# Three moves in the last stage of an adaLN block: the range check's passes, one norm among the gelus, and the order of eight transposes

## The chip, the cores and the metric

The kernel runs on one core of one Trainium2 chip. The metric is the device time of one execution in microseconds (us). One execution was also taken by the hardware profiler; its span, from the first to the last instruction, and all durations below come from that one.

Engines are named as in the profile: PE is TensorE's matmul, PEld its weight load, DVE is VectorE, ACT is ScalarE, POOL is GpSimd, SP is SyncE, which here issues most of the DMAs.

## The reference, cut to what matters

One transformer block with adaptive layer norm, for one sequence of 2048 tokens, width 512, 32 heads of 16, and an MLP of width 1376, all in bf16:

```python
sa, ca, ga, sb, cb, gb = (silu(c) @ w_mod).reshape(6, 512)
h = layernorm(x) * (1 + ca) + sa
q, k, v = split_heads(h @ wqkv)                  # 32 heads of 16
p = softmax(q @ k.T * 16 ** -0.5)
x = x + ga * (merge_heads(p @ v) @ wo)
h = layernorm(x) * (1 + cb) + sb
x = x + gb * (gelu(h @ w1 + b1) @ w2 + b2)
```

## The kernel before, in words

Attention fills nearly all of the time. The 2048 queries are taken in four blocks of 512, and in each block the heads in pairs. Scores, exponentials and the product with V are put in an order by a planner that runs while the kernel is written out: it keeps a clock for each of PE, ACT, DVE and POOL and gives the engine that is free first its next piece. It has nothing to say about the part that is changed here: after its loop (lines 1551 to 1590) the last tokens are finished by the function `last_tail` (line 1602), in an order written out by hand. Each engine runs its own instructions in the order in which they are written, so the order of the lines is the order of each engine's queue.

`last_tail` deals with the last block of 512 tokens. Its first 256 tokens ("first half", columns `hA`) have had their attention, residual and norm already; what is left of them is the MLP. Its last 256 tokens ("second half", `hB`, two tiles of 128 tokens) still need everything from the last head pair's softmax division on. The function weaves the two together:

- `fillers` (line 1623) is a generator with the first half's MLP. Eleven times `up_one` (four matmuls of 256 columns and a gelu on ACT), each followed by two steps of the generator; then 22 "downs", single matmuls of 512 columns, eleven for each of the two tiles of tokens, one a step. `gap(n)` advances it by n steps: n steps in the first phase are n/2 ups, in the second phase n downs. The list `GAPS` (line 101) says how many steps go into each of the places, `GAPS[3]` those just ahead of the second half's norm.
- The second half's residual sums lie in two PSUM banks, `pz[0]` and `pz[1]`. Their mean and variance go to DVE (lines 1661 to 1663) and the root to POOL (`ln_root`, lines 291 and 292). Then (1667 to 1672) DVE works out `nb`, ACT normalizes tile 1 (`hns[1]`, an Identity activation) and DVE tile 0 (`hns[0]`).
- Eight PE transposes (1674 to 1677) turn both tiles into banks `kd` and `kr`: chunk j of tile i. Before the change the loop over j is the outer one. ACT copies chunks 0 and 1 to `h2` (1678), DVE chunks 2 and 3 (1679), which are the input of the second half's ups.
- `gap(GAPS[4])`, then DVE copies the residual sums from PSUM to `xr` (1681, 1682).
- The second half's eleven `up_one` (1683 to 1686), in the middle of which `gap(GAPS[6])` puts 13 fillers; `gap(99)` (1687) puts whatever fillers are left.
- `out_add(0)` and `out_add(1)` (1694): DVE adds the residual of the first half, and SP stores the two tiles.
- `range_flag()` (1696, body from 1711): five passes on DVE over `dall`, which holds all the softmax denominators, reduce it to a column `bad`. PE multiplies `bad` by a column of ones (1697), DVE makes a flag of it (1698), and after the tail a general path is run if the flag isn't zero. With these inputs it isn't run.
- The second half's downs: eleven matmuls for tile 2 into `pz[0]` (1699), and for tile 3 two column halves, each one matmul by the identity for the residual and eleven of 256 columns (1703 to 1709). DVE and ACT copy the results, SP and ACT's queue store them.

The five passes of the range check are these (a sixth DVE instruction, line 1721, sets the column of ones):

```python
nc.vector.tensor_scalar(out=ok, in0=dall, scalar1=2.0 ** 30, scalar2=None, op0=ALU.is_le)      # 1713
nc.vector.scalar_tensor_tensor(out=ok, in0=dall, scalar=256.0, in1=ok, op0=ALU.is_ge, op1=ALU.mult)
nc.vector.tensor_reduce(out=okr, in_=ok, axis=mybir.AxisListType.XY, op=ALU.min)               # 1717
nc.vector.tensor_scalar(out=bad, in0=okr, scalar1=-1.0, scalar2=1.0, op0=ALU.mult, op1=ALU.add)
nc.vector.memset(onec, 1.0)                                                                    # 1721
```

The last row of `dall` comes in by the DMA of line 1660, early in the tail.

Of the kernel before, what the change touches and what calls it, by code (L numbers as in the profile page):

```python
# [26 lines left out]
NC = 4  # L27
# [70 lines left out]
TIE = True  # L98
SEARCH = None
NARROW = False  # L100
GAPS = (4, 2, 2, 17, 2, 3, 13)
NHQ = 4
N2_ENG = DV
NHC = NC - NHQ // 2
# [59 lines left out]
def adaln_block(ctx: ExitStack, tc: tile.TileContext, A_x, A_wqkv, A_wo, B_x, B_w1, B_b1, B_w2, B_b2,  # L164
# [81 lines left out]
    def bank(i):  # L246
        return PS[:, i, :]
# [41 lines left out]
    def ln_root(mv, n):  # L289
        rs = small.tile([P, 4], FP32, name="rs")  # L290
        nc.gpsimd.tensor_scalar(out=rs[:, 0:n], in0=mv[:, 0:n, 1], scalar1=EPS, scalar2=None, op0=ALU.add)  # L291
        nc.gpsimd.tensor_tensor(out=rs[:, 0:n], in0=rs[:, 0:n], in1=mhalf[:, 0:n], op=ALU.pow)
        return rs
# [36 lines left out]
    def copy(eng, dst, src):  # L330
        if eng == AC:
            nc.scalar.copy(out=dst, in_=src)
        else:
            nc.vector.tensor_copy(out=dst, in_=src)
# [1267 lines left out]
    def last_tail():  # L1602
# [13 lines left out]
        def up_one(fc, k, half):  # L1616
            ps = bank(k)[:, 0:256]
            for j in range(NC):
                up_mm(ps, h2 if half else ha, fc, j, hB if half else hA)
            nc.scalar.activation(out=uG[:, fc, hB] if half else ua(fc), in_=ps, func=ACT.Gelu_apprx_tanh, bias=b1c[:, fc:fc + 1],  # L1620
                                 scale=1.0)
# [13 lines left out]
        def gap(n):  # L1635
            for _ in range(n):
                next(gen, None)

        nc.vector.tensor_copy(out=o, in_=bank(kO))
        nc.scalar.activation(out=onec, in_=onec, func=ACT.Gelu_apprx_tanh)  # L1640
        gap(GAPS[0])
        cols = [slice(P * i, P * i + P) for i in range(4)]
# [3 lines left out]
        nc.vector.reciprocal(out=rt.rearrange("p t r -> p (t r)"), in_=bank(kd)[:, 0:16])  # L1646
        gap(GAPS[1])
        for i in (0, 2, 1, 3):
            nc.vector.tensor_copy(out=rx[:, cols[i]].rearrange("p (r e) -> p r e", e=32),
                                  in_=rt[:, i, :].unsqueeze(2).to_broadcast([P, 4, 32]))  # L1650
            nc.tensor.matmul(out=bank(kr)[:, cols[i]], lhsT=rx[:, cols[i]], rhs=ident32, start=True, stop=True)
        gap(GAPS[2])
        for t in range(2):
# [10 lines left out]
        rs = ln_root(mv, 2)  # L1664
        gap(GAPS[3])
        nb = small.tile([P, 2], FP32, name="nb")
# [4 lines left out]
        nc.vector.tensor_scalar(out=hns[0], in0=bank(pz[0]), scalar1=mv[:, 0, 0:1], scalar2=rs[:, 0:1],  # L1671
                                op0=ALU.subtract, op1=ALU.mult)
        both = [PS[:, k, :].bitcast(BF16).rearrange("p (j n) -> p j n", n=256) for k in (kd, kr)]
        for j in range(NC):
            for i in range(2):
                nc.tensor.transpose(out=both[j // 2][:, j, i * P:(i + 1) * P], in_=hns[i][:, j * P:(j + 1) * P],
                                    identity=ident)
        copy(AC, h2[:, 0:2, hB], both[0][:, 0:2, :])
        copy(DV, h2[:, 2:4, hB], both[1][:, 2:4, :])
        gap(GAPS[4])  # L1680
        for t in range(2):
            copy(DV, xr[:, 2 + t, :], bank(pz[t]))
        for fc in range(NFC):
            up_one(fc, (kO, kw, kd, kr)[fc % 4], 1)
            if fc == GAPS[5]:
                gap(GAPS[6])
        gap(99)

        def out_add(tt, k):
            obs[tt] = tl2.tile([P, D], BF16, name="ob")  # L1690
            nc.vector.tensor_tensor(out=obs[tt], in0=bank(k), in1=xr[:, tt, :] if tt > 1 else xa[:, tt, :], op=ALU.add)
            (nc.scalar if tt == 3 else nc.sync).dma_start(out=out_tok[4 * b + tt], in_=obs[tt])

        for tt in range(2):
            out_add(tt, dA[tt])
        bad, onec_, fl = range_flag()
        nc.tensor.matmul(out=bank(kw)[0:1, 0:1], lhsT=bad, rhs=onec_, start=True, stop=True)
        nc.vector.tensor_copy(out=fl, in_=bank(kw)[0:1, 0:1])
        for fc in range(NFC):
# [11 lines left out]
    def range_flag():  # L1711
        ok = odp.tile([P, 512], FP32, name="rb").rearrange("p (q f) -> p q f", f=16)
        nc.vector.tensor_scalar(out=ok, in0=dall, scalar1=2.0 ** 30, scalar2=None, op0=ALU.is_le)
        nc.vector.scalar_tensor_tensor(out=ok, in0=dall, scalar=256.0, in1=ok,
                                       op0=ALU.is_ge, op1=ALU.mult)
        okr = gp.tile([P, 1], FP32, name="okr")
        nc.vector.tensor_reduce(out=okr, in_=ok, axis=mybir.AxisListType.XY, op=ALU.min)
        bad = gp.tile([P, 1], BF16, name="bad")
        nc.vector.tensor_scalar(out=bad, in0=okr, scalar1=-1.0, scalar2=1.0, op0=ALU.mult, op1=ALU.add)
        onec = gp.tile([P, 1], BF16, name="onec")  # L1720
        nc.vector.memset(onec, 1.0)
        fl = gp.tile([1, 1], I32, name="fl")
        late.update(fl=fl)
        return bad, onec, fl
# [104 lines left out]

    scr_d1 = scr.tile([4, 512], FP32, name="d1")  # L1830
    last_tail()
    att.close()
    general_path()
# [35 lines left out]
```

## Time and profile before

| what | us |
|---|---|
| median of 3 runs (lowest to highest) | 757.19 (755.67 to 757.39) |
| the profiled execution's own time | 755.64 |
| its span, first to last instruction | 753.9 |
| PE busy in the span | 734.1 (97%) |
| ACT busy | 721.2 (96%) |
| DVE busy | 676.5 (90%) |
| POOL busy | 415.6 (55%) |
| last exponential of the attention ends | 721.1 |
| `last_tail`'s first instruction starts (DVE, line 1639) | 721.58 |
| last matmul ends | 750.30 |

The profile's rows name an instruction by the line that writes it, its engine, its operation and the tiles it writes and reads (`out<-in`). A line may be that of a helper: all ups and downs of the tail carry line 689, the helper `plain`, and are told apart by their operands: `hT,W` is an up of the first half, `h2T,W` one of the second, `W,hT` a down of the first half, `W,uG` one of the second. Line 1620 is the gelu (`hT` first half, `uG` second), lines 332 and 334 are `copy` on ACT and DVE, line 1691 is `out_add`'s addition, L1676 the transposes. Times are us from the span's start. The duration of a matmul includes the time that its result takes to come out; matmuls that follow each other closely overlap, so that their spacing, start to start, is shorter than their duration.

### The profile page before, as it was taken

Reading aid. Unit: us, or ns where it says so; the run is one execution under the profiler, and the core shown is the slowest. Engines: PE = TensorE matmul, PEld = TensorE weight load, DVE = VectorE, ACT = ScalarE, POOL = GpSimd, SP = SyncE. Lnnn points to the kernel's source line nnn. Section 1 sums busy time; section 2 is a strip of 40 time slices with the busy share of each in tenths; the row PEclk is TensorE's granted clock in tenths of the full one; section 3 lists DMA queues with packets and bytes.
Section 4 is the critical chain, followed back from the end, with each engine's and each line's share of the span. In section 5 each row is a group of like instructions: output and inputs, shape, how many; then the busy total and the mean of one; then the engine's idle time right before and its main releaser. Section 6 shows DMA issues by size and latency. Waiting matters only on the chain.

```text
span 753.9 us, 22023 instructions
## 1 busy us (share of the span) xinstructions
PE 734.1 (97%) x9010; PEld 238.2 (32%) x9010; DVE 676.5 (90%) x1185; ACT 721.2 (96%) x779; POOL 415.6 (55%) x263
## 2 busy tenths in 40 slices
PE   8999999999999999999999999999999999999996
PEld 3322322232333222222222222222222223444454
DVE  6958999999999999899999999999999989898832
ACT  4999999999999999999999999999999999999971
POOL 4103556566675655766556677765756466345700
PEclk9999999999999999999999999999999999999998
DMA  9400000021110110000100200001100200010110
GB/s 318 116 16 2 25 10 17 8 91 38 45 50 10 30 24 18 3 23 23 45 17 18 37 3 17 14 13 30 45 17 9 45 3 17 9 43 19 38 17 31
DMA packets 41964, 25.60 MB, mean 34 GB/s; under 512 B 26705, under 2 KB 37010, under 8 KB 41858
## 3 DMA queue, kind: packets, MB, share of 16 engines
q1 hardware_dynamic: 41042, 23.02, 12.1%
q8 instruction: 72, 1.18, 0.6%
q10 hardware_dynamic: 816, 1.12, 0.4%
q14 instruction: 34, 0.28, 0.1%
HBM read 16.59 MB, written 2.61 MB: 25 GB/s over the span
## 4 chain that ended last, share of the span: by engine, by line
ACT 50%; PE 38%; issue 9%; DVE 1%; POOL 1%; DMA 0%; DVEq 0%; ACTq 0%; POOLq 0%
ACT pB L1300 24%; ACT pA L1300 24%; PE PS L1108 13%; PE PS L944 13%; PE PS L254 8%; PE PS L689 3%; ACT uG L749 1%; POOL t L1348 1%; DMA xb<-in_A_x_dram 0%; PE PS L1125 0%; ACT hT L1620 0%; ACT L1300 0%; DVE st L281 0%; PE PS L311 0%; ACT hT L321 0%
## 5 line engine op out<-in xcount | busy, mean ns | idle before, releaser
L1348 POOL TENSOR_SCALAR t<-t 128x2048 int16<-128x2048 int16 x187 | 353.9, 1901 | 257.5 <-DVE t L1342 149.7
L1300 ACT ACTIVATE pA<-PS 128x1024 bf16<-128x1024 f32 x369 | 395.9, 1073 | 2.6 <-PE PS L944 2.4
L1300 ACT ACTIVATE pB<-PS 128x1024 bf16<-128x1024 f32 x369 | 396.1, 1073 | 0.2
L1371 DVE TENSOR_SCALAR t<-PS 128x512 int16<-128x512 f32 x572 | 369.5, 681 | 25.0 <-PE PS L944 21.1
L944 PE MATMUL PS<-qm,kT 32*128 32x512 bf16 x2048 | 307.5, 383 | 6.7 <-ACT pA L1300 2.7
L1108 PE MATMUL PS<-t,VV 128*32 128x512 f16 (+1 forms) x1944 | 226.9, 359 | 2.5 <-POOL t L1348 1.4
L944 PEld LDWEIGHTS <-kT 32*128 32x128 bf16 x2048 | 85.3, 91 | 289.1 <-issue 285.5
L1342 DVE TENSOR_SCALAR t<-t 128x2048 int16<-128x2048 int16 x242 | 173.0, 742 | 0.5
L1108 PE MATMUL PS<-pA,VE 128*32 128x512 bf16 (+1 forms) x828 | 170.4, 361 | 0.0
L1108 PE MATMUL PS<-pB,VE 128*32 128x512 bf16 (+1 forms) x828 | 166.1, 361 | 0.0
L1108 PE MATMUL PS<-t,VE 128*32 128x512 f16 (+1 forms) x648 | 133.6, 359 | 0.2 <-DVE t L1371 0.2
L1108 PEld LDWEIGHTS <-VE 128*32 128x32 bf16 x2304 | 69.7, 94 | 76.8 <-issue 70.5
L1108 PEld LDWEIGHTS <-VV 128*32 128x32 bf16 x1944 | 64.6, 95 | 55.1 <-issue 50.6
L254 PE MATMUL PS<-h2T,W 128*32 128x512 bf16 x528 | 42.7, 383 | 0.0
L254 PE MATMUL PS<-W,uG 128*32 128x512 bf16 x528 | 41.3, 383 | 0.0
L1125 PE MATMUL PS<-kT,zeros 128*32 128x512 bf16 x288 | 27.8, 383 | 0.0
L341 DVE TENSOR_SCALAR qm<-PS,qmask 128x512 bf16<-128x512 f32 x32 | 22.5, 742 | 3.4 <-PE PS L254 3.4
L740 DVE TENSOR_SCALAR uG<-PS,b1c 128x512 bf16<-128x512 f32 x33 | 24.5, 742 | 1.1 <-PE PS L254 1.1
L1486 POOL TENSOR_TENSOR OT<-o_sb,rb 128x512 bf16<-128x512 f32 (+1 forms) x17 | 20.1, 1179 | 9.4 <-DVE t L1342 7.1
L291 POOL TENSOR_SCALAR rs<-mv 128x4 f32<-128x4 f32 (+1 forms) x10 | 4.3, 432 | 34.8 <-DVE mv L286 34.7
L254 PE MATMUL PS<-hT,W_k 128*32 128x512 bf16 x256 | 20.8, 383 | 1.0 <-DVE hT L324 0.9
L254 PE MATMUL PS<-hT,W_q 128*32 128x512 bf16 x256 | 20.5, 383 | 0.0
(142 smaller groups left out, 376.7 us busy)
## 6 DMA issues: line engine op xcount, KB each, us to landing
rb<-d SPq DMA_DIRECT2D x112, 32.0 KB
W_m<-in_w_mod_dram SPq DMA_DIRECT2D x2, 1024.0 KB
out_dram<-ob SPq DMA_DIRECT2D x15, 128.0 KB
o_sb<-o SPq DMA_DIRECT2D x56, 32.0 KB
xb<-in_A_x_dram SPq DMA_DIRECT2D x3, 512.0 KB
xr<-in_A_x_dram SPq DMA_DIRECT2D x3, 512.0 KB
W<-in_B_w_dram SPq DMA_DIRECT2D x4, 344.0 KB
W<-in_B_w_dram SPq DMA_DIRECT2D x5, 256.0 KB
```

The source lines that it names most:

```text
L254: nc.tensor.matmul(out=ps[32 * g:32 * g + 32, :], lhsT=lhsT[:, 32 * g:32 * g + 32], rhs=rhs, start=start, stop=stop)
L341: nc.vector.tensor_scalar(out=qm[(b, ch)][:, par, :], in0=ps, scalar1=qmask[:, par:par + 1], scalar2=None, op0=ALU.mult)
L689: nc.tensor.matmul(out=ps, lhsT=lhsT, rhs=rhs, start=start, stop=stop)
L740: nc.vector.tensor_scalar(out=X["u"][:, fc, :], in0=bank(ps), scalar1=late["b1c"][:, fc:fc + 1], scalar2=None, op0=ALU.add)
L944: nc.tensor.matmul(out=dst, lhsT=kT[rows, ch, kt * P:(kt + 1) * P], rhs=rhs, start=True, stop=True)
L1108: nc.tensor.matmul(out=bank(O[qi])[32 * r:32 * r + 32, cs], lhsT=w, rhs=rhs[:, cs], start=(n == 1 and not halved(qi)), stop=last and (pr = ...
L1125: nc.tensor.matmul(out=bank(O[qi])[32 * r:32 * r + 32, :], lhsT=zeros[:, 0:32], rhs=kT[:, 0, 0:512], start=False, stop=False)
L1300: nc.scalar.activation(out=t[:, 0:n, :], in_=PS[:, b0:b0 + n, :], func=ACT.Exp, scale=math.log(2.0) / STEP)
L1342: nc.vector.tensor_scalar(out=t16[:, rs, :], in0=d["tile"][:, rs, :], scalar1=float(MJ[j]), scalar2=None, op0=ALU.add)
L1348: nc.gpsimd.tensor_scalar(out=t16[:, rs, :], in0=d["tile"][:, rs, :], scalar1=1.0, scalar2=float(MJ[j]), op0=ALU.mult, op1=ALU.add)
L1371: nc.vector.tensor_scalar(out=d["tile"][:, r:r + n, :], in0=PS[:, i:i + n, :], scalar1=T_BIAS, scalar2=0.0, op0=ALU.add, op1=ALU.max)
L1486: nc.gpsimd.tensor_tensor(out=ot[:, 0:w], in0=o[:, 0:w], in1=rb[:, 0:w], op=ALU.mult)
```

## The change

The fillers ahead of the second half's norm go from 17 steps to 12, and a new gap of 4 steps stands between the norm and the transposes. The loop over the two tiles becomes the outer one in the transposes. `range_flag()` is called after the residual's copies, ahead of the second half's ups, and no longer after `out_add(1)`; the matmul with `bad` stays where it was.

```diff
-GAPS = (4, 2, 2, 17, 2, 3, 13)
+GAPS = (4, 2, 2, 12, 2, 3, 13, 4)
...
         nc.vector.tensor_scalar(out=hns[0], in0=bank(pz[0]), scalar1=mv[:, 0, 0:1], scalar2=rs[:, 0:1],
                                 op0=ALU.subtract, op1=ALU.mult)
         both = [PS[:, k, :].bitcast(BF16).rearrange("p (j n) -> p j n", n=256) for k in (kd, kr)]
-        for j in range(NC):
-            for i in range(2):
+        gap(GAPS[7])
+        for i in range(2):
+            for j in range(NC):
                 nc.tensor.transpose(out=both[j // 2][:, j, i * P:(i + 1) * P], in_=hns[i][:, j * P:(j + 1) * P],
                                     identity=ident)
...
         for t in range(2):
             copy(DV, xr[:, 2 + t, :], bank(pz[t]))
+        bad, onec_, fl = range_flag()
         for fc in range(NFC):
             up_one(fc, (kO, kw, kd, kr)[fc % 4], 1)
...
         for tt in range(2):
             out_add(tt, dA[tt])
-        bad, onec_, fl = range_flag()
         nc.tensor.matmul(out=bank(kw)[0:1, 0:1], lhsT=bad, rhs=onec_, start=True, stop=True)
```

Counted out in steps of the generator: before, 8 steps are taken by the first three gaps (ups 0 to 3), 17 by the gap ahead of the norm (ups 4 to 10 and downs 0 to 2), then 2, 13 and the last 4. After, the gap of 12 takes ups 4 to 9, the new gap of 4 takes up 10 and downs 0 and 1, then come 2, 13 and the last 5. So on ACT the norm of tile 1 stands ahead of the gelu of up 10, where it stood behind it, and one down of 22 moves from ahead of the transposes to the last gap.

## The prediction

> **What bounds the kernel now.** I read the page first, then the chain of work that ended last from 715 us on, the timeline of the tail, its waits, and the clock in short windows.
>
> ```profile
> PE 734.1 (97%) x9010; PEld 238.2 (32%) x9010; DVE 676.5 (90%) x1185; ACT 721.2 (96%) x779; POOL 415.6 (55%) x263
> PEclk9999999999999999999999999999999999999998
> ```
>
> PE and ACT share the bound of the attention, up to 721 us, and nothing of the change lies there. What counts is who sets the pace in the last 33 us, where PE's row of tenths stays full and only the last clock digit is below 9. The chain goes back through PE nearly all the way, with two exits. The first, around the norm:
>
> ```profile
> 727.41 2.64 ACT hT L1620 x6
> ...
> 730.40 0.78 ACT OT L1670
> 731.18 0.05 issue
> 731.23 0.56 PE PS L1676 x7
> 731.79 0.43 PE PS L689 x2
> 732.22 0.02 issue
> 732.24 8.65 PE PS L689 x61
> ```
>
> ACT works off the first half's gelus, only then norms tile 1 (L1670), and PE's transposes wait for that. From 732.24 PE has 8.65 us of matmuls without a break. The second exit follows:
>
> ```profile
> 740.91 0.06 DVE ob L1691
> ...
> 741.52 0.43 DVE rb L1713
> 741.95 0.02 issue
> 741.97 0.70 DVE rb L1714
> 742.67 0.02 issue
> 742.69 0.70 DVE okr L1717
> 743.39 0.02 issue
> 743.41 0.16 DVE bad L1719
> 743.57 0.04 DVE onec L1721
> 743.61 0.04 issue
> 743.65 0.16 PE PS L1697
> 743.81 6.51 PE PS L689 x35
> ```
>
> PE has run out of fillers, DVE adds the last first-half tile, runs the range check, and PE's small matmul L1697 waits for it. PE is in order, so the 35 matmuls of the second half's downs stand behind. The windows show what follows the pause (columns: window, its length, then busy us and count of PE, PEld, DVE, ACT, POOL, then granted clock, DMA share, GB/s):
>
> ```profile
> 740.90:743.65 2.75, 0.00 (x0) 0.00 (x1) 2.56 (x6) 0.00 (x0) 0.00 (x0) 0.92 0.14 48
> 743.65:744.65 1.00, 1.00 (x4) 0.43 (x5) 0.15 (x1) 0.00 (x0) 0.00 (x0) 0.50 0.00 0
> 745.65:746.65 1.00, 1.00 (x3) 0.30 (x2) 0.00 (x0) 0.00 (x0) 0.00 (x0) 0.52 0.00 0
> 746.65:747.65 1.00, 1.00 (x7) 0.51 (x6) 0.00 (x0) 0.00 (x0) 0.00 (x0) 1.00 0.00 0
> ```
>
> The clock is halved at the end of the pause (in shorter windows it is 1.00 up to 743.1 and 0.50 from 743.3) and stays so for the first 3 us of the downs.
>
> **Part 1, the range check.** Removed from the path: the wait. Before, the last filler down starts at 740.49, and downs stand 0.216 apart (739.85, 740.06, 740.28, 740.49), so PE's next slot is 740.71; L1697 starts at 743.65. That is 2.94 us. L1697 itself stays; the first down follows it by 0.10. Its other input is bank kw, last read by gelu 9, and all second-half gelus end by 740.52 (the row of seven from 737.43, 3.09 long), so no wait takes the old one's place.
>
> Added elsewhere: the same six DVE instructions, from 741.52 to 743.57, 2.05 us, behind the residual's copies. These end at 732.17 + 1.28 = 733.45 before, and some 0.47 earlier after (part 3), so the check fills DVE from 733.0 to 735.05. Queued behind it on DVE is the addition of first-half tile 0, whose last down comes out at 735.46 before and 735.2 after: DVE idles 2.03 us in front of it today, and this pause hides the check. The next late thing on DVE is the addition of tile 1 at 740.6. If the cover were gone, a store would start later, and nothing on PE. The passes also wait for `dall`: its DMA (L1660) is issued at 724.56, its 144 packets all lie between 725.4 and 725.9, 7 us ahead. No DMA and no POOL work is moved; the flag's cast now stands behind the addition of tile 1, with nobody waiting before the end.
>
> Gain: 2.94 us.
>
> **Part 2, the clock.** The eleven downs into pz[0] start at 743.75, and the identity matmul after them at 747.52: 3.77 us. At the 0.216 of the first half's downs they would take 2.38. If PE never pauses, the clock doesn't fall, and 1.39 us go. Bounds: 0 if the clock falls all the same, 1.39 at full speed; I take 1.39, since no shorter pause in this tail halves it: the windows from 721 to 740.9 show 1.00 throughout, with PE busy only 1.87 of 2.40 us around the norm. The Trainium skill ("TensorE: Matmul & The Clock Gate", Part 1) says that half clock comes after an idle window of about 3.4 us. Here it came 2.3 us after the last matmul, so the row disagrees with the sentence read literally.
>
> **Part 3, the norm and the transposes.** Gelus of the first half start 0.437 apart, the last at 730.03, and the norm 0.37 behind it. With one gelu fewer ahead, the norm starts behind the gelu of 729.59: 729.96, and ends 0.77 later, 730.73. Its inputs are there: nb starts at 729.19 and takes 0.16. PE by then has done up 10 and downs 0 and 1, slots to 730.26, and the four transposes of tile 0 (ready 729.27 + 0.81 = 730.08), which are 0.057 apart, by 730.49. It then waits for tile 1 as before, from 730.79: 0.44 earlier than 731.23. ACT's copy needs tile 1's chunks 0 and 1: start 730.85, out after 0.22, 731.07, plus 0.04 to notice; in the old order it was the fourth after the wait, now the second, 0.06 more. But ACT runs gelu 10 first: 730.63 to 730.73 by the overlaps seen, end 731.10 to 731.20. So the copy starts between 731.10 and 731.20 (before 731.60), takes 0.59, and the second half's ups start 0.05 behind it, at 731.74 to 731.84 instead of 732.24. DVE's copy (0.42 from 731.22) ends earlier, and PE's two downs of GAPS[4] end their slots by 731.45. Gain 0.40 to 0.50; I take 0.47, near the upper end, since only the start of gelu 10 stands against it.
>
> Cost: one down more in the last gap, 0.216, where PE is dense. Before, it lay in front of the transposes, where PE was waiting anyway. Net gain of part 3: 0.25 us.
>
> The tile order alone is worth the 0.06 above: the four transposes that it takes from behind the wait save 4 x 0.057 = 0.23 for DVE's copy and PE's queue, but ACT's copy is last.
>
> **The sum.** 2.94 + 1.39 + 0.25 = 4.58 us. PE's matmuls end at 745.7 instead of 750.3; what follows (ACT's copy, a store, the end) is 3.6 us and unchanged. The span becomes 749.3, the profiled execution's time 755.64 - 4.58 = 751.1. That execution was 1.55 below the median of the runs, and next to the lowest, 755.67; from the median, 757.19, the sum gives 752.6, which I forecast.
>
> **The rivals.**
>
> - *The clock falls anyway.* If the halving had its own timetable and not the pause as its cause, part 2 goes and 3.2 remain: 754.0. For it: the changes at 743.2 and 746.65 are 3.4 us apart, like ticks of a counter. Against: full clock from 721 to 743. The idle rule of the Trainium skill named above gives this case if 2.9 us is too short a pause to have been the cause.
> - *Part 3 gives nothing.* Gelu 10 gets between norm and copy, or PE's dense stretch is held by the gelus' banks; then the ups start as before and the extra down costs 0.22: 2.94 + 1.39 - 0.22 = 4.1, 753.1. For it: ACT has no slack there. Against: 0.44 per gelu is an even row.
> - *A store holds the last tile.* The output buffer has two slots, so the copy of tile 3 (749.03 before, 744.45 after) waits for the store of tile 1. That store's packets end by 743.2 before, by 742.9 after: 1.5 us of room. It would have to take 1.5 us more to show, and then costs what exceeds that.
> - *The check waits for dall, and all DVE behind it: slower.* Place: L1713, now ahead of the additions and the flag. PE's L1697 starts 2.13 us (743.65 - 741.52) after L1713. It decides against the change when `dall` lands so late that L1697 starts later than before: after 741.5 the gain of part 1 is gone, and at 744.0 the time is 757.19 + 2.5 = 759.7. Against: the packets end at 725.9, 15 us ahead of that point.
> - *The diff doesn't do what it says.* If the matmul with `bad` waited for something else late, time would stay at 757; its two inputs and its bank are listed above, and none is.
>
> **How the numbers follow.** Full sum 0.80 (752.6); part 3 without gain 0.07 (753.1); clock falls anyway 0.05 (754.0); no gain for a reason not seen 0.04 (757); slower through dall or another late input of DVE 0.04 (759.7). The store's case lies inside these. About 0.3%, 2.3 us, is what a measurement of this kernel can tell from no change; the three first cases are all beyond it: faster 0.92, same 0.04, slower 0.04. The range: runs of before reach from 1.5 below the median to 0.2 above, so the likeliest sum spreads from 751.1 to 752.8; the low clock case adds up to 754.0, and a part 3 at its bound of 0.50 lowers the lower end by a little. 750.8 to 754.2.
>
> **What would show it.** Right: no wait of PE for DVE at L1697, the matmul with `bad` at about 740.5; clock 1.00 through the last downs, these 0.216 apart; L1713 to L1721 between 733 and 735.1 and DVE still idle in front of the addition of tile 0; L1670 starting near 729.96, the second half's ups near 731.8; the last matmul's end near 745.7. Wrong: a new wait at L1697, clock 0.50 anywhere before 745, an ACT table load around L1670, ups starting at 732.2, or a last store that starts later than 0.5 us behind its matmul.

## The result, and the profile after

| | us |
|---|---|
| changed kernel, median of 4 runs (lowest to highest) | 751.2 (750.93 to 751.32) |
| kernel before, median of 4 runs (lowest to highest) | 756.48 (755.67 to 757.39) |
| ratio, 95% interval | 0.9929 [0.9912, 0.9947] |
| profiled execution after: own time, span | 751.11, 749.3 |
| last matmul's end, before and after | 750.32 and 745.86 |

The forecast was 752.6, range 750.8 to 754.2; the profiled execution alone was put at 751.1, with its span at 749.3 and the last matmul's end at 745.7. The windows of the changed kernel from the matmul with `bad` to the end of the downs, all at full clock (columns as in the prediction):

```profile
740.40:742.90 2.50, 2.45 (x13) 1.13 (x13) 0.74 (x2) 0.00 (x0) 0.00 (x0) 1.00 0.15 52
742.90:745.80 2.90, 2.90 (x26) 2.29 (x24) 1.12 (x2) 0.00 (x0) 0.00 (x0) 1.00 0.15 51
```

The row of clock tenths on the page is too coarse for this: a digit stands for nearly 19 us, in which 3.4 us at half clock still leave a 9.

The changed kernel's chain of work that ended last, from the norm on (start, length, what):

```profile
730.01 0.11 ACT OT L1670
...
730.67 0.47 ACT hT L1620
731.15 0.01 issue
731.16 0.59 ACT h2T L332
731.75 0.04 issue
731.80 1.91 PE PS L689 x16
733.70 0.05 issue
733.76 6.89 PE PS L689 x45
740.64 0.09 PE PS L1698
740.74 0.75 PE PS L689 x3
741.49 0.05 issue
741.55 4.31 PE PS L689 x31
```

DVE has left the chain: where it stood from 740.91 to 743.65, with the addition and the five instructions of the check, the matmul with `bad` (now L1698) follows the last filler down, and PE runs from 731.80 to 745.86 with no pause above 0.05 us. At the norm, ACT runs norm, gelu 10 and copy in one piece, and on the chain the ups wait for the copy. PE still waits 0.3 us for the norm, at the transposes of tile 1, but this wait is no longer on the chain. Where the range check went, from the timeline (start, length, engine, line, then in brackets DVE's idle time ahead of it):

```profile
732.81 0.41 DVE L1714 TENSOR_SCALAR rb<-dall 128x512 f32<-128x512 f32 x1
...
734.81 0.06 DVE L1722 MEMSET onec<- 128x1 bf16 x1
735.25 0.69 DVE L1693 TENSOR_TENSOR ob<-PS,hT 128x512 bf16<-128x512 f32 x1 [0.38 <-PE PS L689]
```

DVE still idles 0.38 us behind the check, where it idled 2.03 before: the cover held, with that much to spare.

Runs of one kernel fall into groups here, which the runs' mean granted clock tells apart: some executions have one or more further stretches of 3.4 us at half clock, ahead of the tail. One stretch takes 3.4 / 2 / 754 = 0.0023 off the mean clock, which is how the clock tells their number, though not their place. For the kernel before, 28 of the 64 runs made with the experiments have 0.997 or 0.998 (one stretch, by the first profile the tail's own) and a median of 755.8; the other 36 have 0.995 or less and lie between 756.7 and 760.3. Below, "clean" is a run without a further stretch (for the changed kernel, clock 0.999 or 1.000), and next to it stands a length within one trace that no earlier stretch touches: from the start of the gelu of up 4 to the end of the last matmul, "the tail". It is 750.32 - 727.41 = 22.91 before and 745.86 - 727.46 = 18.40 after: 4.51 less.

### The profile page after: what moved, and what is told of

Read it like the earlier page. It is cut to its first block, busy times and chain, and to the rows that moved or that the text cites. A ratio compares the mean times of both kernels' runs of the same rounds, so it can differ in the third digit from the quotient of the medians.

```text
span 749.3 us, 22019 instructions
## 1 busy us (share of the span) xinstructions
PE 732.6 (98%) x9006; PEld 238.1 (32%) x9010; DVE 676.4 (90%) x1185; ACT 721.1 (96%) x779; POOL 415.0 (55%) x263
## 4 chain that ended last, share of the span: by engine, by line
ACT 52%; PE 37%; issue 9%; POOL 1%; DVE 1%; DMA 0%; DVEq 0%; ACTq 0%; POOLq 0%
ACT pA L1300 25%; ACT pB L1300 24%; PE PS L1108 13%; PE PS L944 13%; PE PS L254 8%; PE PS L689 2%; ACT uG L749 1%; POOL t L1348 1%; DMA xb<-in_A_x_dram 0%; ACT hT L1620 0%; ACT L1300 0%; DVE st L281 0%; PE PS L1125 0%; PE PS L311 0%; ACT hT L321 0%
```

## The experiments

Main theory: the gain is the wait for the range check (2.94 us), the half clock that the wait caused (1.39), and the earlier norm less one down (0.25). Rivals: the clock falls anyway; part 3 gives nothing; the gain comes from another place.

**The kernel before again.** No edit.

> The kernel before, unchanged, run again. Its runs so far fall into two groups, 755.7 and 757.2 to 757.4, while those of the changed kernel lie within 0.4 us. Theory: the group is set by how long TensorE stays at half clock after its pause in front of the matmul with bad. Then runs near 755.7 show a mean clock of 0.997 or 0.998 (3.4 us of 754 at half), runs near 757.3 a lower one, by 3.2 us more at half clock 0.995. Rival: the groups come from the attention or the DMAs and have one clock.

Measured: 12 runs from 755.67 to 760.27, in steps: five at 0.997 or 0.998 (755.67 to 755.92), three at 0.995 (757.07 to 757.22), three at 0.993 (758.2 to 758.4), one at 0.991. The clock does set the group, but not by the tail: the profiled execution (757.22) has a further stretch at half clock from about 11.7 to 15.1 us, in the prologue, and its first exponential starts at 15.92, not 14.77. The theory fell as to the place. In this execution the tail is 751.78 - 728.58 = 23.20 long, 0.29 more than in the other profile, because here the clock fell 0.6 us after the downs had begun and all of the stretch lay on them: 4.08 us for eleven downs, where the other had 3.77. So the clock term isn't one number: 1.39 in one execution, 4.08 - 2.38 = 1.70 in the other.

**The range check alone.**

```diff
         for t in range(2):
             copy(DV, xr[:, 2 + t, :], bank(pz[t]))
+        bad, onec_, fl = range_flag()
...
             out_add(tt, dA[tt])
-        bad, onec_, fl = range_flag()
```

> The kernel before with the range check's five passes moved behind the residual's copies, nothing else. Main theory: the wait (2.94 us) and the half clock after it (1.39 in the profiled run) both go: 4.3 us below a 755.7 run of before, so 751.3, last matmul's end near 746.0, no wait at the matmul with bad, clock 1.00 until then. Rival, the clock falls anyway: 2.9 us, 752.7. Rival, the norm carries most of the gain: under 1 us.

Measured: median 751.51; four clean runs from 751.27 to 751.53; ratio 0.9938 [0.9922, 0.9955]. Two more, 752.51 (the profiled one, with a further stretch in the prologue) and 754.1, are not clean. The tail is 747.19 - 728.51 = 18.68: 4.23 of the 4.51 come from this one line. Clock 1.00 through the downs, which are 0.216 apart. The sum of the two terms was 4.33; the 0.1 that is missing lies at the matmul with `bad`, which starts 741.91 - 741.60 = 0.31 behind the last filler down and not 0.216.

**The wait kept, PE kept busy.**

```diff
         bad, onec_, fl = range_flag()
+        for _ in range(13):
+            nc.tensor.matmul(out=bank(kr), lhsT=zeros[:, 0:P], rhs=zeros, start=True, stop=True)
         nc.tensor.matmul(out=bank(kw)[0:1, 0:1], lhsT=bad, rhs=onec_, start=True, stop=True)
```

> The kernel before with 13 matmuls of 512 columns on zeros put on TensorE ahead of the matmul with bad, into a bank that nothing reads later. They take 13 x 0.216 = 2.8 us, so they fit into the pause of 2.94 us; the range check and the wait for it stay. Main theory: the pause is the cause of the half clock, so the clock stays at 1.00 and 1.4 us go without any wait being taken away: 754.3, and the runs form one group only. Rival, the clock falls anyway: 755.7 and two groups as before.

The windows of this kernel, the pause with the extra matmuls and the downs behind it (columns as in the prediction):

```profile
742.30:745.20 2.90, 2.90 (x15) 1.14 (x13) 2.57 (x6) 0.00 (x0) 0.00 (x0) 1.00 0.13 45
745.20:748.00 2.80, 2.80 (x16) 1.46 (x16) 0.27 (x2) 0.00 (x0) 0.00 (x0) 1.00 0.00 0
```

DVE does the check as before (2.57 us of DVE in this window, with the end of the addition), and the matmul with `bad` starts 745.20 - 728.96 = 16.24 us behind the gelu of up 4, as it did before (743.65 - 727.41 = 16.24): the wait is all there. But the clock is 1.00, and the downs run at full speed. The tail is 750.48 - 728.96 = 21.52, 1.39 less than before, the very size of the clock term; clean runs are at 754.14 to 754.29, as expected. Against the 755.8 of the kernel before this is 1.6, nearer to the 1.70 of its second profile. Three of eleven runs are clean; the other eight, at 0.998, have one stretch each (in the profiled one it is in the prologue again; where it lies in the other seven no profile shows), so that part of the expectation was wrong for the reason just found. Ratio 0.9981 [0.9972, 0.9990]. None of the 64 runs with the pause left empty has a mean clock above 0.998. The pause causes the half clock: "the clock falls anyway" is out.

**A shorter pause.** The check reads only the last 2 of the 32 rows of `dall`.

```diff
-        nc.vector.tensor_scalar(out=ok, in0=dall, scalar1=2.0 ** 30, ...
+        nc.vector.tensor_scalar(out=ok, in0=dall[:, NQ - 2:NQ, :], scalar1=2.0 ** 30, ...
```

(and likewise in the second pass, with `ok` cut to 2 rows)

> The kernel before with the range check over the last 2 of the 32 rows of denominators; the other 30 are left out of it. The three long passes (0.42, 0.69, 0.69 us on 512 columns) shrink to some 0.1 each, so the pause goes from 2.94 to about 1.5 us and 1.4 us go at once. Open between the theories: if a pause of 1.5 us is too short to halve the clock, another 1.4 go (752.9); if any pause can do it, by where a window of some 3.4 us happens to end, runs fall into two groups about 1.4 us apart or more, 752.9 and 754.3.

Measured: two clean runs, 752.94 and 753.28, and four at 0.997 from 753.93 to 754.41, of which the profiled one has its stretch in the prologue; for the other three no profile shows whether it lies there or in the tail. PE's pause is 743.50 - 741.80 = 1.70 us, clock 1.00 throughout, tail 748.79 - 728.50 = 20.29: 2.62 less than before, of which the shorter wait gives 2.94 - 1.70 = 1.24 and the clock 1.38. The three long passes had been put too low (0.17 to 0.19 us each, not 0.1).

**A pause in between.** The same cut with 16 rows of 32.

> The kernel before with the range check over 16 of the 32 rows of denominators; the other 16 are left out of it. The passes on 256 columns take some 0.28, 0.42 and 0.42 us, so the pause is about 2.25 us, between the 2.94 that halved the clock and the 1.53 that did not in any run. The time falls by 0.7 at once. If the pause's length alone decides with a limit of about 3 us, the clock stays and all runs without another half-clock stretch lie near 753.6 with clock 1.000; if what decides is how much of a window of 3.4 us the pause takes, some runs fall (755.0, 0.998) and some don't.

Measured: 11 runs, all at 0.998 or less, eight of them from 755.03 to 755.27 or at 754.46; ratio 0.9987 [0.9977, 0.9998]. The pause lasts from 740.72 to 743.00, 2.28 us, and the profiled execution shows the fall (same columns):

```profile
740.75:743.00 2.25, 0.14 (x1) 0.00 (x1) 1.90 (x6) 0.00 (x0) 0.00 (x0) 1.00 0.16 58
743.00:743.40 0.40, 0.40 (x3) 0.27 (x4) 0.15 (x1) 0.00 (x0) 0.00 (x0) 1.00 0.00 0
...
743.80:744.00 0.20, 0.20 (x2) 0.06 (x1) 0.00 (x0) 0.00 (x0) 0.00 (x0) 0.80 0.00 0
...
745.40:746.60 1.20, 1.20 (x5) 0.36 (x4) 0.00 (x0) 0.00 (x0) 0.00 (x0) 0.50 0.00 0
...
747.40:748.00 0.60, 0.60 (x8) 0.54 (x6) 0.53 (x1) 0.00 (x0) 0.00 (x0) 1.00 0.00 0
```

The clock is full during the pause and falls 0.9 us after work has begun again; it comes back 3.4 us later. A limit near 3 us is out: 2.28 us halved it. The pause of 1.70 us did not, in one profile and two runs. (The 1.53 of the expectation is that same pause, counted from the end of the last matmul; 1.70, 2.28 and 2.94 are counted from PE's next slot.) That the clock falls some time behind the end of the pause, and not at it, speaks for the share of a window, but doesn't show it. The expected mix of falling and not falling runs was not seen with certainty; only the run at 754.46 could be one of the second kind.

**The norm put back.**

```diff
-GAPS = (4, 2, 2, 12, 2, 3, 13, 4)
+GAPS = (4, 2, 2, 17, 2, 3, 13, 0)
```

> The changed kernel with the fillers as before (17 steps ahead of the norm, none behind it); range check and transposes as changed. Main theory: the norm of tile 1 stands behind the gelu of up 10 again, so it starts 0.44 later, near 730.45; the second half's ups start 0.43 later than in the changed kernel (731.80), and one down less stands in the last gap (0.22): 0.2 us slower, 751.4 in runs with clock 1.000. Rival, part 3 gives nothing: ups start at the same place and the time is 0.2 us lower.

Measured: one clean run, 751.22, and four at 0.998 (752.5 to 753.1), so the time tells nothing. The trace does: from the gelu of up 4, the ups of the second half start 733.46 - 728.68 = 4.78 later, against 4.34 in the changed kernel, and the tail is 747.30 - 728.68 = 18.62, 0.22 more. That is the expected 0.2. Part 3 is real, and small.

**The old order of the transposes.** The two loop lines exchanged in the changed kernel.

> The changed kernel with the transposes in the old order (chunk outer, tile inner). Main theory: ACT's copy waits for the third transpose after the norm instead of the second, but gelu 10 ends at about the same time, so the ups start 0.05 later at most; DVE's copy ends 0.2 later, near 731.87, still ahead of the third matmul of the first up: 751.2 to 751.3, nothing that a time can tell. Rival, the order carries part 3: ups 0.2 or more later, 751.4.

Measured: three clean runs from 750.96 to 751.20, two others at 752.55 and 753.84; the tail 748.63 - 730.18 = 18.45, 0.05 more than in the changed kernel. By itself the order is worth 0.05 us, below what a time can show.

**The check one step earlier.**

```diff
         copy(AC, h2[:, 0:2, hB], both[0][:, 0:2, :])
+        bad, onec_, fl = range_flag()
         copy(DV, h2[:, 2:4, hB], both[1][:, 2:4, :])
...
-        bad, onec_, fl = range_flag()
```

> The changed kernel with the range check's passes one step earlier: on DVE ahead of its copy of the transposed chunks, and no longer behind that and the residual's copies. Main theory: the passes are free only where DVE has nothing that PE waits for. DVE is free from 730.13 and its copy could start at 731.27; the passes take 2.05, so the copy ends near 732.65 instead of 731.69, the ups of the second half wait at their third matmul (732.03 in the changed kernel) until 732.7: 0.7 us slower, 751.9 in runs with clock 1.000. Rival, any place ahead of the last downs is as good: 751.2.

From this kernel's timeline, DVE's copy and the matmuls of the second half's ups that wait for it:

```profile
734.77 0.42 DVE L334 COPY h2T<-PS 128x512 bf16<-128x512 bf16 x1
...
735.25 1.69 PE L689 MATMUL PS<-h2T,W 128*128 128x256 bf16 x14 [0.32 <-DVE h2T L334]
```

The wait is where it was expected, at the third matmul, but the loss is 0.47 (tail 749.08 - 730.21 = 18.87), and the four clean runs are at 751.39 to 751.48, 0.3 above the changed kernel's (the fifth, 754.51, has a further stretch). DVE's copy ends at 735.19, which is 732.44 in the changed kernel's times, and so 0.2 earlier than worked out. The place matters: 2 us of DVE are free behind the copy and not ahead of it.

**The changed kernel again.** No edit.

> The changed kernel, unchanged, run again. Its 4 runs so far all show a mean clock of 0.999 or 1.000; of 35 runs of the kernel before, 17 show about 0.998 (755.6 to 756.2 us), 11 show 0.995 (756.7 to 757.6), 6 show 0.993 and one 0.991. A profile at 0.995 had a second stretch of 3.4 us at half clock at 11.7 to 15 us, in the prologue, which the change doesn't touch, and everything after it 1.2 us later. If the prologue is the cause of the groups, the changed kernel must show them as well: most runs near 751.2 with clock 1.000, the others 1.1 to 1.6 us later with 0.998. If the change had removed them, all runs lie near 751.2.

Measured: 751.01, 751.16, 751.17, and two with a further stretch, 752.01 and 752.29: the change doesn't remove the groups, its first four runs had only met none. Ratio 0.9932 [0.9919, 0.9945]. The profiled execution (752.01) has its stretch neither in the prologue nor in the tail but in the attention, where the trace shows waits of PE of about 0.2 us and no longer ones:

```profile
414.00:414.40 0.40, 0.36 (x4) 0.15 (x3) 0.40 (x2) 0.40 (x2) 0.00 (x0) 1.00 0.00 0
...
417.50:418.00 0.50, 0.50 (x7) 0.14 (x8) 0.27 (x2) 0.04 (x2) 0.45 (x1) 0.50 1.07 214
```

**More downs into the pauses.**

```diff
-GAPS = (4, 2, 2, 12, 2, 3, 13, 4)
+GAPS = (4, 2, 2, 12, 4, 3, 13, 4)
...
         for i in range(2):
+            gap(i)
             for j in range(NC):
```

> The changed kernel with one filler down between the transposes of tile 0 and those of tile 1, and four in place of two behind them, all taken from the last gap. PE waits 0.3 us at the first place (730.53 to 730.84) and 0.5 us at the second (731.29 to 731.80). Main theory: the first down is hidden, the two others push the ups from 731.80 to 731.93, and three downs of 0.216 leave the dense stretch: 0.52 less, 750.7 in runs with clock 1.000. Rival, the copies of ACT and DVE are held up by the downs: no gain, 751.2.

The chain of this kernel around the transposes is PE alone:

```profile
730.74 0.22 PE PS L1678 x4
730.96 0.22 PE PS L689
731.18 0.33 PE PS L1678 x4
731.51 2.61 PE PS L689 x20
```

Tail 745.62 - 727.73 = 17.89, 0.51 less than the changed kernel; clean runs 750.42, 750.44 and 750.81. It is faster than both kernels where no further stretch falls into it; the median of its 6 runs, three of them with one, is 751.19; ratio to the kernel before 0.9934 [0.9921, 0.9948].

**Matmuls on zeros in the prologue, alone and with those downs.**

```diff
         mod_col(bank(6), W_m0, D, m, 4 + m)
+    warm(4)
```

> The changed kernel with four matmuls of 512 columns on zeros in the prologue, behind the modulation's matmuls and ahead of the first projection, where TensorE idles 0.9 us (10.36 to 11.26). In five of the seven profiles with clock 0.998 or less ahead of the tail, the clock fell to half there. Main theory: that pause, with 0.9 us of one-column matmuls ahead of it, is the cause of most of the groups, so fewer runs show 0.998, and the best ones stay at 751.2. Rival: nothing changes, since in two profiles the half clock came in the middle of the attention without a pause; then about half of the runs show 0.998 or less as before.

> The two last edits together: the downs moved from the last gap into the pauses around the second half's transposes, and the four matmuls on zeros in the prologue. Main theory: 0.5 us below the changed kernel, 750.6 in most runs, and so faster than both kernels in the median as well. Rival: the groups are as before and the median lies near 751.5.

Measured, alone: four clean runs (751.0 to 751.31) and three at 0.995 (753.9 to 754.9); ratio 0.9950 [0.9931, 0.9968]. With the downs: four clean (750.75 to 751.0), two not (753.7, 755.11); median 750.99, ratio 0.9945 [0.9925, 0.9964]. Inconclusive: 8 of 13 runs are clean, for the changed kernel 7 of 9, and the profiled executions of both happened to be clean, so they don't show where the others fell. That no run of the 13 has exactly one further stretch of moderate cost (0.997 or 0.998), where eight of eleven had with the pause filled in the tail alone, is a hint and no more.

## Why the prediction was right, point by point

- **Part 1, the wait, 2.94.** Right. The matmul with `bad` starts at 740.58 ("about 740.5"), 0.1 behind PE's next slot, and no other wait took the old one's place; the check lies at 732.81 to 734.87 ("between 733 and 735.1"), and DVE idles 0.38 us behind it. Alone, the moved line gives 4.23 of tail, with the clock term in it, where the two terms make 4.33.
- **Part 2, the clock, 1.39.** Right in cause and size for the execution it was read from: filling the pause alone gave 1.39. The rival of a clock that falls anyway is refuted by that run. The term isn't fixed, 1.70 in another execution; that the two figures of 1.39 agree to the digit is luck of where the stretch began in the profile that was read.
- **Part 3, the norm, 0.25.** Right: 0.22 for the gaps and 0.05 for the order when each is undone. The norm starts at 730.01 ("near 729.96"), ACT's copy at 731.16 ("between 731.10 and 731.20"), the ups at 731.80 ("near 731.8").
- **The sum, 4.58.** Measured in the tail, 4.51, which is 4.23 for the moved check and 0.28 for the rest; between the two profiled executions' own times, 755.64 - 751.11 = 4.53.
- **The step that was off: the start.** The forecast put the sum on the median of three runs, 757.19. Two of those three runs lie at 756.7 or above, where every run with a known clock had 0.995 or less, which is at least one further stretch; the profiled execution, which was read, had none. Put on that one, the same sum gives 751.1, and the changed kernel's first four runs, all without such a stretch, have a median of 751.2. Clean against clean, 755.8 and 751.16, the difference is 4.6. The two medians of the table differ by 5.28, because two of the four runs before lie in that upper group and none of the four after has a further stretch. That draw was luck: two of the next five runs of the changed kernel had one. So the measured median's place in the range says little; the sum is borne out by the tail and the single edits. I noted that the profiled execution was 1.55 below the median and didn't ask why three runs should lie at 755.67 and at 757.19 and 757.39.
- **The slower rival** (the check waiting for `dall`) didn't happen: the first pass started right behind the residual's copies. Nor did the rival of the store: the last copy starts at 745.88, 0.02 behind the last matmul, and its store is issued 0.40 us later, as before (750.34 and 750.75).
- **Two readings that were off and changed no term.** The check is five DVE instructions, four passes and the `memset`, and not six; the sixth in the window from 740.90 is the addition ahead of them. And in the old order the first transpose of tile 0 ran ahead of the wait, at 730.47, so that ACT's copy waited for the third transpose behind it, not the fourth, and the new order takes three transposes from behind the wait, 0.17 us, not four and 0.23.

## What to carry to other kernels

In this kernel a wait of 2.94 us in front of a dense stretch of matmuls cost its length, and 1.39 to 1.70 us more by the half clock behind it; a small result that only a late instruction needs belongs on its engine behind the last thing that TensorE waits for and ahead of that engine's next pause, and one step too early costs again. If runs of one kernel fall into groups, compare their mean granted clock first, and put a sum worked out in one execution on that execution's time, not on a median of others.

## What the runs showed of the hardware that was not expected

- The half clock comes in stretches of 3.4 us: 743.19 to 746.61 in the kernel before, 745.55 to 748.96 in its second profile, 743.92 to 747.34 with half the check, 415.1 to 418.5 in the attention (the ends by the mean clock of short windows). One stretch, seen in two profiles (234 to 241), was twice as long.
- It can begin during the pause or up to 0.9 us after it. A pause of 1.70 us didn't halve the clock in the execution profiled and two clean runs; one of 2.28 us did in the profile, and no run of that kernel showed a mean clock above 0.998. In the 3.4 us ahead of each fall PE was idle for 2.3 us (fall at 743.19), 2.7 (745.55) and 2.1 (743.92, half the check); the pause that halved nothing was 1.5 us of idle time. A limit on the idle share of such a window, between 1.5 / 3.4 = 0.45 and 2.1 / 3.4 = 0.62, would fit these four; it is an estimate that no run tested. The Trainium skill ("TensorE: Matmul & The Clock Gate", Part 1) describes a free-running window of 3413 ns, which agrees with the length and with falls behind the pause; that half clock comes after an idle window of about 3.4 us, as it also says, doesn't agree with 2.28 us.
- Stretches of half clock also came in the prologue (five profiles), starting between 10.7 and 11.7 us, during or behind a pause of only 0.9 us with one-column matmuls ahead of it, and in the middle of the attention: at 415 us in one profile, with waits of PE of about 0.2 us, and from 234 to 241 in two, with PE busy for 5.95 of the 6 us ahead of them in both. An idle share doesn't explain those; what triggers them stays open.
